# The last twelve attention slots of a linear-attention and cosine-MLP kernel: 64 tokens of two batches instead of 128 tokens of one

## The chip, the core and the metric

The kernel runs on one core of a Trainium2 chip. The time is the device time of one execution in microseconds (us). Three executions of the kernel before took 512.67, 513.03 and 513.1 us, a median of 513.03 us. The engines that matter are TensorE (PE in the profile, its weight loads PEld), VectorE (DVE), ScalarE (ACT), GpSimd (POOL) and SyncE (SP), which issues most DMAs. The two on-chip memories are SBUF and PSUM; PSUM has 8 banks, and matmuls write only there.

## The reference

Four batches of eight heads, 768 tokens, head size 48. A linear attention with a decaying state runs along the tokens, and its output, 3072 tokens by 384 features, goes through an MLP with 2048 inner features and the gate h·cos(h):

```python
for t in range(S):
    kt, vt, rt = (k[:, :, t], v[:, :, t], r[:, :, t])
    cur = np.einsum('bhd,bhe->bhde', u[None] * kt, vt)
    y[:, :, t] = np.einsum('bhd,bhde->bhe', rt, state + cur)
    state = w[None, :, :, None] * state + np.einsum('bhd,bhe->bhde', kt, vt)
...
h = x @ w_in
g = h * np.cos(h)
return (g @ w_out).astype(np.float32)
```

All inputs are float32. The tokens of a batch are chained by the state; the four batches don't depend on each other.

## The kernel before

**Slots.** The 3072 tokens are cut into 24 slots of 128 tokens. Slot `i` holds chunk `i // 4` of batch `i % 4` (`chunk`, L656). Within a slot the recurrence is done with matmuls. Keys and queries are scaled by powers of the decay relative to the middle of the chunk (`decT_k`, `decT_r`), so that the product of a key and a query carries the right power of `w`. For one slot TensorE does:

- `mm_a` (L814, matmul L819): for each of four head pairs `p` and both heads `j` of a pair, scores of 128 keys by 128 queries, with a contraction over 48 numbers. The two heads lie in different halves of the array's rows. VectorE's `mask` (L826) then copies the scores above the diagonal over a diagonal matrix that ScalarE has written (`diagonal`, L809: the bonus `u`).
- `mm_x` (L835, matmul L840): 12 matmuls of the queries with the state, each giving 32 output features, in four column parts of the array.
- `mm_x2` (L844, matmul L853): 16 matmuls of the masked scores with the values, again 32 features each.
- `mm_z` (L871, matmul L875): 8 matmuls of scaled keys and values, which give the slot's addition to the state. VectorE's `state` (L927) adds and scales it; the last chunk of a batch needs none.

All of these are float32 matmuls, and each of them is two MATMUL instructions in the profile. The result is split into a high and a low part (`xh`, `xl`) for the MLP.

**Early and late slots.** Slots 0 to 11 (`i < XS`, `XS = 12`) transpose keys and queries on TensorE (L730). Slots 12 to 23 are "late": they are worked off between matmuls of the MLP. Their keys and queries come through staging buffers `raw` with four DMAs each (`load_s`, L690), are transposed by VectorE in 32x32 blocks (L738) and scaled by GpSimd (L743). Late slots issue `mm_x`, `mm_x2` and `mm_z` as one run on TensorE (`mm_xz`).

**The MLP.** Eight blocks of three slots (384 tokens). A step does one group of 128 inner features of a block: 9 float32r matmuls 128x128 by 384 columns for `h` (`mm_h`, L316), the cosine gate on ScalarE and VectorE, and 9 matmuls of the same size for the output (`mm_o`, L322). There are 128 steps, so 2304 such matmuls. Blocks 0 to 3 go in four rounds over parts of the features, blocks 4 to 7 go through all 16 groups at once. A block's first step needs all three of its slots.

**PSUM.** Banks 0 to 2 hold the outputs of the MLP (`B_ACC`), 3 and 4 the values `h` (`B_H`; in blocks 0 to 3 also bank 5, `B_HX`), 5 to 7 the attention (`B_ATT`). Early slots may use all but bank 2 (`B_EARLY`).

**What sets the order.** Every operation is an `Op` with an engine, a due time, a cost and the buffers it uses. `Plan.order` runs 61 passes of list scheduling with changed due times, replays each order with jittered costs, and keeps the one that ends first. Instructions are then issued in that order: an engine's order is fixed when the program is built. `Tile` is one buffer, `Buf` a use of one, and `_free_at` tells when a buffer is free. Of the operations that can start at the same time, an engine takes the one that is due first; it does not leave itself idle for one that is due earlier but starts later. SP's order holds also for its DMAs: one that waits for a buffer holds up those behind it.

## Time and profile before

| | |
|---|---|
| median of three executions | 513.03 us |
| the profiled execution | 512.26 us |
| its span, first to last instruction | 510.5 us |
| TensorE busy | 501.5 us (98%) |
| VectorE busy | 381.0 us (75%) |
| ScalarE busy | 331.0 us (65%) |
| GpSimd busy | 177.1 us (35%) |
| mean granted TensorE clock | 0.999 |

The busy time of TensorE is the time in which at least one matmul is recorded as running. Matmuls overlap, so their durations add up to more than the span; how long one holds up the next is seen from the starts of neighbouring rows in the timeline. A row of the timeline gives the start, the time from the first start to the last end, the engine, line and operation, and the number of instructions merged into the row. In the notation `48*128 48x128` the first pair is rows by columns of the array that are in use, the second the partitions and columns of the moving operand.

### The profile page before, as it was taken

The page shows a single profiled execution, that of the slowest core. Times are in us where ns is not written, and L with a number is a line of the kernel's source. Part 1 is how long each engine was busy: PE and PEld are TensorE (multiplying, and loading weights), DVE is VectorE, ACT ScalarE, POOL GpSimd, SP SyncE. Part 2 cuts the span into 40 slices and gives each one's busy share as a digit, 9 for nine tenths or more (in the row PEclk, how much of TensorE's full clock was granted, in tenths as well). Part 3 has the DMA queues.
Part 4 walks back from the last instruction along what each step waited for, and adds up shares of the span by engine and source line. Part 5 has one row for each costly group of instructions (what it writes and reads, how often), then busy time and mean ns, then how long its engine had stood idle before and what let it go on. Part 6 is the DMA issues. An engine that isn't in the chain of part 4 may idle for free.

```text
span 510.5 us, 11742 instructions
## 1 busy us (share of the span) xinstructions
PE 501.5 (98%) x4389; PEld 480.0 (94%) x4389; DVE 381.0 (75%) x773; ACT 331.0 (65%) x833; POOL 177.1 (35%) x184
## 2 busy tenths in 40 slices
PE   8999999999999999999999999999999999999995
PEld 5788899999999999999999999999999999999995
DVE  6898999888888875576777777777777767756553
ACT  2989987767667756556657465575665765655453
POOL 6777422445454451242426224224044041300000
PEclk9999999999999999999999999999999999999999
DMA  8999226586666593524676736446455465200001
GB/s 137 179 179 190 79 86 218 152 167 156 157 140 131 127 180 44 76 65 67 160 146 151 159 99 167 111 156 152 105 130 140 142 170 114 89 16 33 1 1 49
DMA packets 114975, 61.56 MB, mean 121 GB/s; under 512 B 78433, under 2 KB 110818, under 8 KB 114914
## 3 DMA queue, kind: packets, MB, share of 16 engines
q1 hardware_dynamic: 109586, 53.50, 42.7%
q0 software_dynamic: 5184, 7.08, 9.9%
q8 instruction: 35, 0.57, 0.5%
q14 instruction: 26, 0.21, 0.2%
q10 hardware_dynamic: 144, 0.20, 0.1%
HBM read 48.96 MB, written 11.80 MB: 119 GB/s over the span
## 4 chain that ended last, share of the span: by engine, by line
PE 94%; DMA 2%; DVE 1%; ACT 1%; issue 1%; POOL 0%; SPq 0%; DVEq 0%; POOLq 0%; ACTq 0%
PE bank L322 41%; PE bank L316 39%; PE bank L819 4%; PE bank L853 4%; PE bank L840 3%; PE bank L875 2%; PE bank L730 1%; DMA v<-in_v_dram 1%; DMA k<-in_k_dram 1%; ACT A L809 1%; PE bank L1094 0%; DVE pq L440 0%; POOL f L765 0%; DVE a L800 0%; DVE rq L447 0%
## 5 line engine op out<-in xcount | busy, mean ns | idle before, releaser
L322 PE MATMUL bank<-w_out_hi,gh 128*128 128x384 f32 x384 | 131.9, 344 | 0.0
L322 PE MATMUL bank<-w_out_hi,gl 128*128 128x384 f32 x384 | 129.8, 338 | 0.0
L316 PE MATMUL bank<-xh,w_in_lo 128*128 128x384 f32 x384 | 129.7, 338 | 0.0
L322 PE MATMUL bank<-w_out_lo,gh 128*128 128x384 f32 x384 | 129.5, 337 | 0.0
L316 PE MATMUL bank<-xh,w_in_hi 128*128 128x384 f32 x384 | 129.1, 336 | 0.0
L316 PE MATMUL bank<-xl,w_in_hi 128*128 128x384 f32 x384 | 128.8, 335 | 0.0
L330 DVE SCALAR_TENSOR_TENSOR f<-bank,qi 128x384 f32<-128x384 f32 (+1 forms) x132 | 71.4, 543 | 47.0 <-ACT qi L327 46.5
L327 ACT ACTIVATE qi<-bank 128x384 int32<-128x384 f32 (+1 forms) x132 | 62.8, 479 | 57.7 <-PE bank L316 57.0
L1033 ACT CAST gh<-f 128x384 fp32r<-128x384 f32 (+1 forms) x132 | 65.7, 500 | 48.9 <-DVE f L1030 46.9
L1030 DVE TENSOR_TENSOR f<-bank,f 128x384 f32<-128x384 f32 (+1 forms) x132 | 71.2, 542 | 32.5 <-ACT f L333 30.3
L1036 DVE TENSOR_TENSOR gl<-f,gh 128x384 fp32r<-128x384 f32 (+1 forms) x132 | 80.7, 613 | 19.6 <-ACT gh L1033 19.1
L333 ACT ACTIVATE f<-f 128x384 f32<-128x384 f32 (+1 forms) x132 | 67.3, 513 | 41.6 <-DVE f L330 40.8
L322 PEld LDWEIGHTS bank<-w_out_hi,gh 128*128 128x128 f32 x384 | 72.0, 188 | 3.0 <-issue 0.8
L316 PEld LDWEIGHTS bank<-xh,w_in_lo 128*128 128x128 f32 x384 | 72.2, 188 | 0.3 <-DVE w_in_lo L631 0.3
L316 PEld LDWEIGHTS bank<-xh,w_in_hi 128*128 128x128 f32 x384 | 72.2, 188 | 0.3 <-issue 0.2
L316 PEld LDWEIGHTS bank<-xl,w_in_hi 128*128 128x128 f32 x384 | 72.1, 188 | 0.0
L322 PEld LDWEIGHTS bank<-w_out_hi,gl 128*128 128x128 f32 x384 | 72.1, 188 | 0.0
L322 PEld LDWEIGHTS bank<-w_out_lo,gh 128*128 128x128 f32 x384 | 72.0, 188 | 0.0
L809 ACT ACTIVATE A<-ident,a 128x128 f32<-128x128 f32 x192 | 59.6, 391 | 4.9 <-DVE a L800 4.8
L743 POOL TENSOR_TENSOR kT<-kT,decT_k 112x512 f32<-112x512 f32 x12 | 15.6, 1301 | 129.3 <-DVE kT L738 74.4
L621 POOL TENSOR_TENSOR f<-f,raw 128x384 int32<-128x384 int32 x32 | 36.7, 1148 | 60.8 <-DVE f L610 31.7
L1078 POOL DMA_DIRECT2D out_dram<-f x36 | 32.7, 1012 | 40.6 <-DVE f L1030 17.2
(88 smaller groups left out, 589.5 us busy)
## 6 DMA issues: line engine op xcount, KB each, us to landing
raw<-in_moe_w_in_dram SPq DMA_DIRECT2D x32, 384.0 KB, 3.2
raw<-in_moe_w_out_dram SPq DMA_DIRECT2D x32, 384.0 KB, 3.2
out_dram<-f POOLq DMA_DIRECT2D x36, 192.0 KB, 4.5
k<-in_k_dram SPq DMA_DIRECT2D x24, 192.0 KB, 4.2
v<-in_v_dram SPq DMA_DIRECT2D x24, 192.0 KB, 5.1
raw<-in_k_dram SPq DMA_DIRECT2D x47, 96.0 KB, 3.1
raw<-in_r_dram SPq DMA_DIRECT2D x47, 96.0 KB, 2.1
out_dram<-f SPq DMA_DIRECT2D x23, 192.0 KB, 1.9
```

The costliest lines, as they stand in the source:

```text
L316: nc.tensor.matmul(ph, a, b_, start=(i == 0), stop=(i == len(mm) - 1))
L322: nc.tensor.matmul(acc, a[:, ts], b_[:, f, :], start=(first and i == 0), stop=(last and i == 2))
L327: nc.scalar.activation(qi, ph, AF.Copy, scale=INV_2PI, bias=0.25)
L330: nc.vector.scalar_tensor_tensor(q, ph, INV_2PI, qi, op0=ALU.mult, op1=ALU.subtract)
L333: nc.scalar.activation(q, q, AF.Sin, scale=TWO_PI, bias=0.5 * math.pi)
L621: lambda: nc.gpsimd.tensor_tensor(ai(), ai(), cn(), op=ALU.add),
L809: nc.scalar.activation(A[j]()[:, p, :], ident, AF.Copy, scale=ab()[:, h : h + 1])
L819: nc.tensor.matmul(cube(Ap[j])[:, p, :], kT()[ps, p, :], rT()[ps, p, :], start=True, stop=True)
L1030: nc.vector.tensor_tensor(g()[:, cs], ph()[:, cs], q()[:, cs], op=ALU.mult)
L1033: nc.scalar.copy(gh()[:, cs], g()[:, cs])
L1036: nc.vector.tensor_tensor(gl()[:, cs], g()[:, cs], f32(gh())[:, cs], op=ALU.subtract)
L1078: nc.gpsimd.dma_start(dst, ob(), accum_op=ALU.add)
```

## The change

The twelve late slots get a function of their own, `late_chunk`. A late slot now holds 64 tokens of two batches, `2m` and `2m + 1`, where `m` alternates between slots: slot 12 is tokens 384 to 447 of batches 0 and 1, slot 13 the same tokens of batches 2 and 3, slot 14 tokens 448 to 511 of batches 0 and 1, and so on. In a half of the partitions (`half[b]`) lie the tokens of one batch. The number of slots, and the 384 columns that each block of the MLP streams, stay as they are.

- The score matmuls of a slot become 16 of 48x64 with 64 moving columns, in four parts of the array (head `j` by batch `b`). The addition to the state becomes 16 matmuls of 64x64, also in four parts. Both are issued as one run, `mm_az`. Ten late slots compute an addition to the state instead of eight.
- The matmuls with the state become 24 of 112x32 with 64 moving columns, those with the values 32 of 64x32 with 64 moving columns, in eight parts of the array; their order is written out in `rounds`. They are one run, `mm_xx`.
- The two PSUM buffers of a slot, `sp` (scores and state) and `xp` (output), are pairs of banks, 5 and 6 or 6 and 7 (`P_ATT`), since the parts in different rows of the array write different banks. The planner learns of buffers made of parts (`Tile.parts`).
- Masks and diagonals are 64 columns wide (`upper2`, `ident2`, made once by GpSimd in `start_late`); the state of two batches is one tensor and is updated in two operations on 384 columns instead of 192.
- Staged loads take eight DMAs instead of four, the other loads two instead of one; the number of bytes is the same.
- The table `dec_k` is made a second time for the 64-token slots (`late_table`: eight matmuls of 128x64 and a copy), after all early slots have used the first. `wr` shares the memory of `dec_k`.
- The early slots keep their code; the last of them scale the state to the middle of a chunk of 64.

```diff
+    CT = C // 2
...
-        bank = [Tile(banks.tile([P, 512], F32, name=f"bank{i}")) for i in range(8)]
+        bank_all = banks.tile([P, 8, 512], F32, name="bank")
+        bank = [Tile(bank_all[:, i]) for i in range(8)]
+        P_ATT = [Tile(bank_all[:, i : i + 2], bank[i : i + 2]) for i in (5, 6)]
...
-        zc = [att.tile([KP, NP, D], F32, name=f"zc{b}") for b in range(B)]
-        R_zt = ring("zt", 2, [KP, NP, 2 * D], F32)
-        wr = att.tile([NP, 2, DP], F32, name="wr")
+        zc = [att.tile([KP, 2, NP, D], F32, name=f"zc{m}") for m in range(NM)]
+        zt = att.tile([KP, 2, NP, 2 * D], F32, name="zt")
+        R_zt = [Tile(zt[:, n]) for n in range(2)]
+        R_zt2 = [Tile(zt, R_zt)]
...
+        wr = dec_k.rearrange("q h d -> q (h d)")[0:NP, 0 : 2 * DP].rearrange("q (j d) -> q j d", j=2)
...
+        def start_late():
+            nc.gpsimd.tensor_tensor(ident2, ident[:, 0:CT], ident[:, CT:C], op=ALU.add)
+            nc.gpsimd.tensor_copy(upper2[0:CT], upper[0:CT, 0:CT])
+            nc.gpsimd.tensor_copy(upper2[CT:P], upper[CT:P, CT:C])
...
+        o_late = op(POOL, 60, 0.6, start_late, [o_pool, o_pool2], port=True)
...
+        def late_table():
+            b_tab2 = Buf(B_ATT)
+
+            def tab_t2():
+                pt = b_tab2().rearrange("q (p t) -> q p t", p=NP)
+                for p in range(NP):
+                    for b in range(2):
+                        nc.tensor.matmul(pt[b * CT : (b + 1) * CT, p, :], decT_k[:, p, mid], ident, start=True, stop=True)
+
+            def tab_copy2():
+                pt = b_tab2().rearrange("q (p j d) -> q (p j) d", p=NP, j=2)
+                nc.scalar.copy(dec_k, pt[:, :, 0:D])
+
+            o_t2 = op(PE, 110, 0.5, tab_t2, [o_tt], [b_tab2], lat=0.3)
+            return op(ACT, 110.5, 0.45, tab_copy2, [o_t2, *early_kd], [b_tab2])
...
+            if i >= XS:
+                return late_chunk(i, due, xbuf)
...
-            def mm_xz():
+            def mm_xx():
                 if c:
                     mm_x()
                 mm_x2()
-                if more:
...
+        def late_chunk(i, due, xbuf):
+            if not o_dk2:
+                o_dk2.append(late_table())
+            m, n_ = (i - XS) % NM, (i - XS) // NM
+            t0 = EC * C + n_ * CT
+            kb, vb, mb, ab, rb = Buf(R_k), Buf(R_v), Buf(R_f), Buf(R_a), Buf(R_f)
+            ks, rs = Buf(R_raw), Buf(R_raw)
+            kT, rT = Buf(R_kT), Buf(R_rT)
+            A = [Buf(R_A) for _ in range(2)]
+            sp, xp, zb = Buf(P_ATT), Buf(P_ATT), Buf(R_zt2)
+            half = [slice(b * CT, (b + 1) * CT) for b in range(2)]
+            more = i < NJ - NM
...
+                def go():
+                    for n in range(4):
+                        for b in range(2):
+                            if i < NJ - 1 or n < 3 or b == 0:
+                                part(n, b, 0, 16, 0, NP, 4 * D)
...
+            ahead = [last_A[0]]
+            l_ks = op(SP, due - 6.2, 3.9, load_s(ks, k), ahead, [ks], lat=3.0, line="late")
+            l_rs = op(SP, due - 6.1, 3.9, load_s(rs, r), ahead, [rs], lat=3.0, line="late")
+            l_k = op(SP, due - 5.2, 1.3, load(kb, k), ahead, [kb], lat=2.6, line="late")
+            l_r = op(SP, due - 5.1, 1.3, load(rn, r), ahead, [rb], lat=2.6, line="late")
+            l_v = op(SP, due - 5.0, 1.3, load(vb, v), ahead, [vb], lat=2.6, line="late")
...
+            def mm_az():
+                for p in range(NP):
+                    for j in range(2):
+                        ps = slice(j * DP, j * DP + D)
+                        for b in range(2):
+                            nc.tensor.matmul(
+                                score(j)[half[b], p, :],
+                                kT()[ps, p, half[b]],
+                                rT()[ps, p, half[b]],
+                                start=True,
+                                stop=True,
+                            )
+                if not more:
+                    return
+                z = z_of()
+                for p in range(NP):
+                    for j in range(2):
+                        for b in range(2):
+                            nc.tensor.matmul(
+                                z[j * DP : j * DP + DP, b, p, :],
+                                kb()[half[b], 2 * p + j, :],
+                                vb()[half[b], 2 * p + j, 0:D],
+                                start=True,
+                                stop=True,
+                            )
+
+            last_A[0] = o_A = op(
+                PE,
+                due - 1.7,
+                1.3 if more else 0.75,
+                mm_az,
+                [e_k, e_r] + ([o_kd, l_v] if more else []),
+                [kT, rT, sp] + ([kb, vb] if more else []),
+                lat=0.3,
+            )
+
...
+                    w_c = pq[0:KP, None, :, 15:16].to_broadcast([KP, 2, NP, D])
+                    nc.vector.tensor_tensor(zc[m], z_of()[0:KP], zc[m], op=ALU.add)
+                    nc.vector.tensor_tensor(zc[m], zc[m], w_c, op=ALU.mult)
+
+                last_z2[m] = op(DVE, due - 1.2, 1.2, state, [o_A, *o_zt, *before, o_pow], [sp])
...
+            def mm_xx():
+                x = xp()[:, :, 0 : NK * CT].rearrange("q b (kk t) -> q b kk t", kk=NK)
+                for kk in range(NK):
+                    for b in range(2):
+                        for g in range(4 * kk, 4 * kk + 4):
+                            p, s = divmod(g, 3)
+                            gs = slice(G * (g % 4), G * (g % 4) + G)
+                            nc.tensor.matmul(
+                                x[gs, b, kk, :],
+                                zb()[:, b, p, G * s : G * s + G],
+                                rT()[0:KP, p, half[b]],
+                                start=(kk == 0),
+                                stop=False,
+                                skip_group_check=True,
+                            )
+
+                rounds = (
+                    ((0, 0), (1, 0), (2, 0), (3, 0)),
+                    ((4, 0), (1, 1), (6, 0), (7, 0)),
+                    ((4, 1), (5, 0), (10, 0), (7, 1)),
+                    ((8, 0), (9, 0), (10, 1), (11, 0)),
                 )
+                for group in rounds:
+                    for b in range(2):
+                        for g, n in group:
+                            p, s = divmod(g, 3)
+                            gs = slice(G * (g % 4), G * (g % 4) + G)
+                            parts = {0: ((0, 0),), 1: ((0, G), (1, D)), 2: ((1, DP + 16),)}[s]
+                            j, at = parts[n]
+                            nc.tensor.matmul(
+                                x[gs, b, g // 4, :],
+                                vb().rearrange("q h d -> q (h d)")[half[b], p * 2 * DP + at : p * 2 * DP + at + G],
+                                A[j]()[half[b], p, 0:CT],
+                                start=False,
+                                stop=(n == len(parts) - 1),
+                                skip_group_check=True,
+                            )
+
+            xo = op(PE, due - 0.7, 1.8, mm_xx, [e_r, l_v, *e_A, *o_zt], [rT, xp, vb, zb, *A], lat=0.3)
...
```

More of the change, by code (lines that the diff above doesn't have):

```diff
@@ L95, in _free_at @@
     def _free_at(tile):
-        if tile.owner is None:
-            return 0.0
-        if any(o.end is None for o in tile.owner.users):
-            return None
-        return max(o.end + o.lat for o in tile.owner.users)
+        t = 0.0
+        for x in tile.parts:
+            if x.owner is None:
+                continue
+            if any(o.end is None for o in x.owner.users):
+                return None
+            t = max(t, max(o.end + o.lat for o in x.owner.users))
+        return t
     def _ready(self, o):
@@ L110, in _ready @@
             for tl in b.tiles:
-                if id(tl) in taken:
+                if any(id(x) in taken for x in tl.parts):
                     continue
@@ L117, in _ready @@
                 return None
-            taken.add(id(best[1]))
+            taken.update(id(x) for x in best[1].parts)
             picks.append((b, best[1]))
@@ L136, in latest @@
             for b in o.bufs:
-                owners = tiles.setdefault(b.tile, [])
-                if not owners or owners[-1][0] is not b:
-                    if all(b is not x for x, _ in owners):
-                        owners.append((b, o))
+                for part in b.tile.parts:
+                    owners = tiles.setdefault(part, [])
+                    if not owners or owners[-1][0] is not b:
+                        if all(b is not x for x, _ in owners):
+                            owners.append((b, o))
         for owners in tiles.values():
@@ L156, in replay @@
             for b in o.bufs:
-                if owner.get(b.tile) is not b:
-                    prev[b] = owner.get(b.tile)
-                    owner[b.tile] = b
-                if prev.get(b) is not None:
-                    t = max(t, max(end[d] + d.lat for d in prev[b].users))
+                if b not in prev:
+                    prev[b] = [owner[x] for x in b.tile.parts if x in owner]
+                    for x in b.tile.parts:
+                        owner[x] = b
+                for a in prev[b]:
+                    t = max(t, max(end[d] + d.lat for d in a.users))
             if o.eng != "PE":
@@ L202, in one_pass @@
                 for tl in b.tiles:
-                    tl.owner = None
+                    for x in tl.parts:
+                        x.owner = None
         nxt, left = {}, {}
@@ L234, in one_pass @@
             for b, tl in picks:
-                b.tile, tl.owner = tl, b
+                b.tile = tl
+                for x in tl.parts:
+                    x.owner = b
             o.gap = t - free[o.eng]
@@ L787, in chunk @@
                 o_kd = op(e2, due - 2.7, c2, decay_k, [o_m, o_dk], [kb], port=True)
-            if not first and not late:
+            early_kd.append(o_kd)
+            if not first:
                 t_k = op(PE, due - 2.5, 0.49, tr(kTp, kb), [o_kd, o_pool], [kb, kTp, kT], lat=0.3)
@@ L935, in chunk @@
-                if not late:
-                    zo = op(PE, due + 1.2, 0.5, mm_z, [o_kd, l_v, o_A], [kb, vb, zp], lat=0.3)
-                last_z[b] = op(
-                    DVE, due + 1.4, 0.3 if c == 0 else 0.65, state, [zo, *o_zt, last_z[b], o_pow], [zp]
-                )
+                    w_c = pq[0:KP, None, :, 15:16].to_broadcast([KP, 2, NP, D])
+                    nc.vector.tensor_tensor(zc[m], z_of()[0:KP], zc[m], op=ALU.add)
+                    nc.vector.tensor_tensor(zc[m], zc[m], w_c, op=ALU.mult)
@@ new lines, in late_chunk, with xv, xo_ @@
+            xo = op(PE, due - 0.7, 1.8, mm_xx, [e_r, l_v, *e_A, *o_zt], [rT, xp, vb, zb, *A], lat=0.3)
+            def xv():
+                return xp()[:, :, 0 : NK * CT].rearrange("q b (kk t) -> q kk b t", kk=NK)
+            def xo_(n):
+                return xbuf()[n].rearrange("q kk (b t) -> q kk b t", b=2)
+            x_h = op(ACT, due - 0.4, 0.47, lambda: nc.scalar.copy(xo_(0), xv()), [xo], [xp, xbuf])
+            x_l = op(
+                DVE,
+                due - 0.2,
+                0.55,
+                lambda: nc.vector.tensor_tensor(xo_(1), xv(), f32(xo_(0)), op=ALU.subtract),
+                [x_h],
+                [xp, xbuf],
+            )
@@ L1057 @@
                     jc = FIRST[n] + t
-                    row = (jc % B) * S + (jc // B) * C
-                    dst = out[row : row + C, :]
+                    if jc < XS:
+                        row = (jc % B) * S + (jc // B) * C
+                        dst = out[row : row + C, :]
+                    else:
+                        m, at = (jc - XS) % NM, EC * C + (jc - XS) // NM * CT
+                        dst = out.rearrange("(b s) d -> b s d", b=B)[2 * m : 2 * m + 2, at : at + CT, :]
                     def cp(acc=acc[t], ob=ob, t=t):
```

226 lines of the change are left out of this document (131 added, 95 removed).

## The prediction

> **What bounds the kernel now.** I read the page first, then busy times by stretch, then the chain of waits, and last the timeline of TensorE around one late slot. From the page:
>
> ```profile
> span 510.5 us, 11742 instructions
> PE 501.5 (98%) x4389; PEld 480.0 (94%) x4389; DVE 381.0 (75%) x773; ACT 331.0 (65%) x833; POOL 177.1 (35%) x184
> ```
>
> The busy time of each engine by stretch (columns: time and count of TensorE, its weight loads, VectorE, ScalarE, GpSimd, then clock, DMA share, GB/s):
>
> ```profile
> 0.00:20.00 20.00, 16.66 (x204) 12.32 (x206) 14.09 (x34) 10.23 (x30) 14.43 (x30) 1.00 0.97 146
> 20.00:60.00 40.00, 39.63 (x765) 34.04 (x763) 36.58 (x70) 37.08 (x110) 28.86 (x28) 1.00 0.87 153
> 60.00:460.00 400.00, 400.00 (x3172) 388.82 (x3171) 304.74 (x611) 260.92 (x642) 133.81 (x127) 1.00 0.54 129
> ```
>
> From 60 to 460 us, where all late slots lie, TensorE is never without a matmul. A busy TensorE needn't be at its peak, so I compare starts. Two rows of the chain of waits that are one step of the MLP apart, and in it nothing else:
>
> ```profile
> 146.18 1.58 PE bank L322 x9
> 149.32 1.58 PE bank L322 x9
> ```
>
> A step is 3.14 us for 18 matmuls, 0.174 us from start to start. Against this the timeline of TensorE around slot 18 (start, time from first start to last end, number of instructions):
>
> ```profile
> 341.71 0.34 PE L322 MATMUL bank<-w_out_lo,gh 128*128 128x384 f32 x1
> 341.98 1.16 PE L819 MATMUL bank<-rT,kT 48*128 48x128 f32 x16
> 343.07 0.44 PE L322 MATMUL bank<-w_out_hi,gh 128*128 128x384 f32 x1
> 343.36 0.34 PE L322 MATMUL bank<-w_out_hi,gl 128*128 128x384 f32 x1
> ...
> 346.15 0.34 PE L322 MATMUL bank<-w_out_lo,gh 128*128 128x384 f32 x1
> 346.42 0.86 PE L840 MATMUL bank<-rT,zt 112*32 112x128 f32 x24
> 347.10 1.08 PE L853 MATMUL bank<-A,v 128*32 128x128 f32 x32
> 348.11 0.56 PE L875 MATMUL bank<-v,k 128*48 128x48 f32 x16
> 348.61 0.45 PE L322 MATMUL bank<-w_out_hi,gh 128*128 128x384 f32 x1
> 348.89 0.34 PE L322 MATMUL bank<-w_out_hi,gl 128*128 128x384 f32 x1
> ```
>
> The reader is to see that the attention sits as two runs between matmuls of the MLP, with no wait in brackets behind any of them. So time that a run no longer takes from TensorE comes off the end, as long as no other engine becomes late. A run's price is the distance between the MLP matmul before it and the second one after it, less two MLP steps of 0.174 (the first matmul after a run is also followed late). The scores cost 343.36 - 341.71 - 0.35 = 1.30 us, the second run with the state's addition 348.89 - 346.15 - 0.35 = 2.39. One of the last four slots, which have no such addition:
>
> ```profile
> 384.92 0.34 PE L322 MATMUL bank<-w_out_lo,gh 128*128 128x384 f32 x1
> 385.19 0.86 PE L840 MATMUL bank<-rT,zt 112*32 112x128 f32 x24
> 385.87 1.08 PE L853 MATMUL bank<-A,v 128*32 128x128 f32 x32
> 386.88 0.45 PE L322 MATMUL bank<-w_out_hi,gh 128*128 128x384 f32 x1
> 387.17 0.33 PE L322 MATMUL bank<-w_out_hi,gl 128*128 128x384 f32 x1
> ```
>
> That is 387.17 - 384.92 - 0.35 = 1.90. All twelve late slots cost 8 x (1.30 + 2.39) + 4 x (1.30 + 1.90) = **42.3 us** of TensorE.
>
> **What a run costs after.** The terms are the time from one round to the next (a round is one instruction on every part of the array) and the fixed time around a run. Mean durations of single instructions, from the groups by line and form:
>
> ```profile
> L819 PE MATMUL bank<-rT,kT 48*128 48x128 f32 x384 | 27.6, 284 | 0.3 <-ACT kT L790 0.2
> L853 PE MATMUL bank<-A,v 128*32 128x128 f32 x768 | 26.8, 275 | 0.9 <-DVE A L826 0.8
> L840 PE MATMUL bank<-rT,zt 112*32 112x128 f32 x480 | 17.2, 277 | 0.0
> L875 PE MATMUL bank<-v,k 128*48 128x48 f32 x320 | 11.1, 212 | 0.2 <-DMA v<-in_v_dram 0.2
> ```
>
> A float32 matmul is two instructions (L819: 24 slots x 8 matmuls, 384 instructions). The run of L840 has 24 instructions on four column parts, 6 rounds: (0.86 - 0.28) / 5 = 0.117 us a round for 128 moving columns. L853 gives (1.08 - 0.275) / 7 = 0.115, the scores, two parts, (1.16 - 0.284) / 7 = 0.125. L875, two parts and 48 moving columns, gives (0.56 - 0.21) / 7 = 0.050. So a round is nearly proportional to the columns. A round with 64 isn't in the trace; it lies between 0.050 and 0.117, and on the line between them at 0.050 + 16/80 x 0.067 = **0.063**, which I take, since 64 is nearest to 48.
>
> Around a run: 0.27 into it (341.98 - 341.71); out of it, from its last instruction's start, 0.15 after L875 (348.61 - 348.46) and 0.20 after L853 (386.88 - 386.68), so 0.16 for 64 columns; 0.29 to the next matmul (343.36 - 343.07); less 0.35: 0.37. Where a run changes the shape of the parts I take 0.16 as for the way out.
>
> - Scores and state in one run, 64x64 parts, four at once: 32 + 32 instructions are 8 rounds at 0.063 and 8 at 0.050, 15 steps: 0.50 + 0.35 + 0.37 = 1.22. Without the state: 7 x 0.063 + 0.37 = 0.81.
> - Output run: 48 instructions of 112x32 on four column parts, 12 rounds, then 64 of 64x32 on eight parts, 8 rounds: 11 x 0.063 + 0.16 + 7 x 0.063 + 0.37 = 1.66. The matmuls with the state gain nothing (12 rounds of 0.063 for 6 of 0.117), since their 112 rows leave no second half; the gain is in the scores and in the values.
>
> Ten slots at 2.88 and two at 2.47 make **33.7 us**, 8.6 less than before.
>
> **What it adds.** The second `dec_k` is 8 matmuls of 128x64, two parts, 8 rounds of 0.117: 0.27 + 0.82 + 0.20 + 0.29 - 0.35 = 1.2 us if it lies in dense work, nothing if the list scheduler puts it where TensorE has nothing else. The latter is likely: it needs only the first table, and the rows just behind that show gaps filled by warm-up matmuls (L1094):
>
> ```profile
> 8.11 0.66 PE L472 MATMUL bank<-ident,decT_k 128*128 128x128 f32 x4 [0.69 <-DVE decT_k L456]
> ...
> 9.30 0.49 PE L1094 MATMUL bank<-warm 128*128 128x256 bf16 x3
> 10.09 0.62 PE L730 MATMUL bank<-ident,r 128*112 128x128 f32 x4 [0.30 <-DMA r<-in_r_dram]
> ```
>
> I take 0.6. But there it would hold one of seven early PSUM banks until its copy, which waits for the last early `decay_k`:
>
> ```profile
> 54.20 1.02 POOL L773 TENSOR_TENSOR k<-k,dec_k 128x384 f32<-128x384 f32 x1
> ```
>
> The early part gets a new order in any case, as the search sees other operations. What it can gain is bounded by TensorE's idle time, 3.3 us in the first 20 and 0.4 in the next 40; I allow 0.5. What it can lose has no row; a loss as large as all of that idle time is 3.7. I take 1.3 of loss, between the ends.
>
> **What lies beside TensorE.** In 60 to 460 us VectorE is busy 76%, ScalarE 65%, GpSimd 33%, and TensorE waits for none of them. The operations that answer to the changed ones, in 230 to 450 us:
>
> ```profile
> L809 ACT ACTIVATE A<-ident,a 128x128 f32<-128x128 f32 x85 | 26.6, 390 | 1.3 <-DVE a L800 1.3
> L826 DVE COPY_PREDICATED A<-upper,bank 128x512 f32<-128x512 int32 x22 | 15.0, 735 | 2.1 <-PE bank L819 2.0
> L919 DVE TENSOR_TENSOR xl<-bank,xh 128x384 fp32r<-128x384 f32 x11 | 6.0, 549 | 1.3 <-ACT xh L914 1.3
> L932 DVE TENSOR_TENSOR zc<-bank,zc 112x192 f32<-112x192 f32 x7 | 2.5, 355 | 3.4 <-PE bank L875 3.4
> ```
>
> Masks of half the width save VectorE some 24 x 0.3 = 7 us, and the wider state (two operations of 0.55 as L919 in ten slots for two of 0.355 in eight) adds 11.0 - 5.7 = 5. Diagonals get shorter, spreads longer, GpSimd does as many operations and 0.6 us once. At no cost, hidden behind TensorE. SP issues more:
>
> ```profile
> 378.58 1.76 SPq L693 DMA_DIRECT2D raw<-in_k_dram  x4
> ...
> 384.74 0.38 SPq L672 DMA_DIRECT2D k<-in_k_dram  x1
> ...
> 402.94 2.44 SPq L693 DMA_DIRECT2D raw<-in_k_dram  x4
> ```
>
> Eight staged DMAs for four are 3.5 us instead of 1.75, twice a slot, and three more loads of some 0.5: 5 us more in the 24 between two slots. Behind them queue the raw weights of the range check, whose result TensorE turns (L555) at 465.63, 45 us before the end:
>
> ```profile
> 465.63 0.27 PE L555 MATMUL bank<-ident,fine 128*1 128x128 f32 x1
> ```
>
> So these 45 us cover it; if they didn't, SP's 12 x 5 us would appear.
>
> **The sum.** The profiled execution took 512.26 us, 0.77 below the median shown. 512.26 - 8.6 + 0.6 + 1.3 = 505.6; on the median's scale **506.3 us**.
>
> **Rivals.**
>
> *The parts don't run at once (slower).* No row has halves of the rows and of the columns in use together. For full overlap speaks that each alone works: the four column parts of L840 take 0.32 us together where one takes 0.277, and the first two instructions of L819, on the two row parts, 0.38 where one after the other would take 0.57:
>
> ```profile
> 346.42 0.32 PE L840 MATMUL bank<-rT,zt 112*32 112x128 f32 x4
> ...
> 341.98 0.38 PE L819 MATMUL bank<-rT,kT 48*128 48x128 f32 x2
> ```
>
> If four 64x64 parts went like two and eight 64x32 like four, scores, state and values would need 8 rounds more each: 8 x (0.063 + 0.050 + 0.063) = 1.41 in ten slots, 1.01 in two, 16.1 us in all: 522.4. It decides once 6.7/16.1 = 42% of that overlap is missing. The Trainium skill (TensorEngine Tiling (Array Packing), Tiling Modes) has tiles load weights and multiply independently in every mode, which is the forecast's side; no row of this trace shows the mixed modes. Chance 5%.
>
> *A larger fixed part in every instruction.* Over a full slot 26 steps are 64-column rounds, 310 over all slots, so each 0.01 us on a round costs 3.1. The scores' round, 0.125, is 0.008 above L840's; if all 64-column rounds have that on top, 0.071, the sum loses 2.5: 508.8. The gain is gone at 0.063 + 6.7/310 = 0.085. Against it stands L875's 0.050, where two parts of 48 columns leave 0.01 beside the moving columns. Chance 8%, at 509. The Trainium skill (TensorEngine Tiling (Array Packing), Instruction Overhead) warns of just this, some 60 cycles per matmul, and advises not to tile a dimension that is already small; at the 2.4 GHz that its page Trainium Kernel Development and Optimization gives (NeuronCore Architecture) that is an estimated 0.025 us, by which 64 columns would take 0.071 and 48 columns 0.060. The trace's 0.050 is below that, and the measurement decides.
>
> *A new wait for PSUM.* Both pairs of banks contain bank 6, so the output run can't start before masks and state update have read the scores' pair. VectorE's part of that is two masks of some 0.4 and two operations of 0.55, 1.9 us, and the MLP takes most of VectorE beside it. Today 3.35 us lie between the two runs (343.07 to 346.42). The planner can place the output run a step later at no cost, since slots are some 20 us apart; only where VectorE is later than planned does TensorE stand. At 0.7 us in ten slots the gain is gone: 513. Chance 7%.
>
> *The early part loses more*, by the held bank or a worse draw of the search: 3.7 us instead of 1.3, 508.7. Chance 12%.
>
> **How the numbers follow.** Forecast 68%, the rivals 5, 8, 7 and 12%. The range: downward, rounds at 0.050 would give 310 x 0.013 = 4.0 more, and the table and the early part 1.9; both ends at once are unlikely, and about half of them gives 503.4. Upward it takes in the fixed part and the early loss together with a little of a wait: 511.0. A difference of 0.2%, 1.0 us, is about what a measurement of this kernel can tell from no change. Slower are the first rival and half of the third with a rest: 9%; within 0.2% the other half: 4%; faster 87%.
>
> **What would show it.** Right: runs of `48*64` with 64 columns beside `64*64`, 1.2 us by the same distance; output runs of `112*32` and `64*32`, 1.66 us; no bracket behind either; TensorE busy throughout from 60 us on; late slots at 34 us in all. Wrong: 16 rounds where I count 8; rounds far from 0.063; a wait for VectorE ahead of the output run; MLP matmuls that stop for the gate; the first step of the MLP's steady part later than before by more than 2 us, which puts it on the early part; the check's matmul near the end.

## The result and the profile after

The changed kernel takes 550.76 us in the median of six executions (548.43 to 551.95), against 513.07 (512.67 to 513.32) for the kernel before: a ratio of 1.0736, 95% interval 1.0719 to 1.0752. The forecast was 506.3 in a range up to 511.0, so it is wrong by its sign. The profiled execution took 550.94 us, its span is 549.2, 38.7 more than the 510.5 before.

**The runs on TensorE came out nearly as forecast.** From the timeline of TensorE after, a run of scores and state, then an output run:

```profile
370.51 0.34 PE L331 MATMUL bank<-xh,w_in_lo 128*128 128x384 f32 x1
370.78 0.69 PE L1040 MATMUL bank<-rT,kT 48*64 48x64 f32 x32
371.30 0.63 PE L1053 MATMUL bank<-v,k 64*64 64x48 f32 x32
371.86 0.44 PE L337 MATMUL bank<-w_out_hi,gh 128*128 128x384 f32 x1
372.14 0.34 PE L337 MATMUL bank<-w_out_hi,gl 128*128 128x384 f32 x1
...
375.98 0.34 PE L337 MATMUL bank<-w_out_lo,gh 128*128 128x384 f32 x1
376.25 0.88 PE L1102 MATMUL bank<-rT,zt 112*32 112x64 f32 x48
377.06 0.86 PE L1124 MATMUL bank<-A,v 64*32 64x64 f32 x64
377.85 0.44 PE L337 MATMUL bank<-w_out_hi,gh 128*128 128x384 f32 x1
378.12 0.34 PE L337 MATMUL bank<-w_out_hi,gl 128*128 128x384 f32 x1
```

By the prediction's distance, 372.14 - 370.51 - 0.35 = 1.28 us (forecast 1.22) and 378.12 - 375.98 - 0.35 = 1.79 (forecast 1.66). Without the state a run costs 0.83 (forecast 0.81). Where no wait stands beside them, twelve slots cost 10 x (1.28 + 1.79) + 2 x (0.83 + 1.79) = 35.9 us: 6.4 less than before, where 8.6 were forecast.

**But TensorE is no longer busy throughout.** The waits of TensorE (engine, buffer and line, what was waited for; us in total, times, longest), after:

```profile
PE bank L331 <- DVE f L1240: 9.3, 6, 5.5
PE bank L1102 <- DVE A L1072: 7.3, 4, 2.5
PE bank L815 <- ACT kT L786: 1.9, 2, 1.2
...
PE bank L1040 <- POOL rT L987: 1.2, 2, 1.0
```

Before, TensorE had no wait after 60 us. Now the MLP waits for the gate's product (L1240) and the output run for the masked scores (L1072). Both are VectorE's, which is busy only 70% of the span. So VectorE was held up itself. To see where, I compare the start of the k-th of the 2304 MLP matmuls in the two traces (after minus before, us):

```
k            145    865   1009   1441   1513   1657   1801   1873   2089   2304   end of span
difference  +2.96  +2.93  +1.71  +1.74  +4.98  +6.71  +8.99  +17.5  +25.9  +27.4       +38.7
```

The early part loses 3.0 us. From the 865th to the 1441st matmul the difference falls only by 1.2. Then there are steps up at 340 to 360, 405 to 430 and 475 to 500 us, which lie just behind the ends of blocks 4, 5 and 6, and 11.3 us come after the last matmul. At those four places the output is stored. DMA traffic from 530 us to the end, after (GB/s in 40 slices, packets, then the queue of ScalarE's one store):

```profile
GB/s 0 0 34 0 0 0 13 13 62 46 29 25 41 51 48 51 48 51 51 48 48 52 45 51 51 51 51 51 51 48 48 51 51 38 13 0 0 0 0 0
DMA packets 394, 0.63 MB, mean 33 GB/s; under 512 B 6, under 2 KB 390, under 8 KB 390
...
q10 hardware_dynamic: 130, 0.20, 2.7%
```

The same view before, from 500 us to the end:

```profile
GB/s 0 0 0 0 0 0 0 0 0 0 0 0 0 0 62 0 0 0 0 0 0 316 392 223 398 345 408 146 18 35 49 12 0 0 0 0 0 0 0 0
DMA packets 436, 0.63 MB, mean 60 GB/s; under 512 B 48, under 2 KB 432, under 8 KB 432
...
q10 hardware_dynamic: 144, 0.20, 5.3%
```

The last three stores, nearly all of the 0.63 MB in both, move at some 50 GB/s instead of up to 400. The queue's packets tell why: 144 are 128 rows and 16 packets of 4 bytes; 130 are 128 rows and 2 such packets. The store is one DMA into `out[2m:2m+2, at:at+64, :]` (L1273), whose outermost dimension is 2, and it runs on **2 DMA engines of 16**: from 536 to 543 us, where only the stores move, the 16 engines are busy 0.13 of the time on average, which is two of them. The Trainium skill states this rule (DMA: Bandwidth & Descriptors, Why a DMA increments its semaphore by 16 and not by 1): the number of engines is the largest up to 16 that divides the slowest dimension of both sides that isn't 1. The trace agrees. Neither this line of the diff nor that rule had a place in the prediction.

What a slow store does in the middle of the kernel is shown by the chain of waits after, around the end of block 6:

```profile
478.50 0.51 SPq L1290
479.01 0.05 issue
479.06 9.97 DMA f<-in_w_dram
489.06 0.36 DVE f L543
...
490.49 0.55 DVE f L1240
491.03 0.04 issue
491.08 3.25 PE bank L331 x9
494.32 2.62 PE bank L337 x9
496.94 1.57 PE bank L331 x9
```

A load of 1.5 KB, the flag of the range check (L539), takes 10 us. It is issued behind three stores, whose packets end at 488.6 us, and lands as they end; in the run below with the stores in two, VectorE doesn't wait for it at all. VectorE's next operation in its order works on that flag (L543), the gate's product stands behind it, and TensorE behind that. Elsewhere VectorE waits for the stores' buffer itself (first two lines; the third is the flag):

```profile
DVE f L578 <- DMA out_dram<-f: 6.2, 3, 3.7
...
DVE f L345 <- DMA out_dram<-f: 5.7, 5, 1.9
DVE f L543 <- DMA f<-in_w_dram: 5.7, 1, 5.7
```

And the longer stalls are paid a second time: after the 5.5 us wait in this chain nine matmuls take 3.25 and 2.62 us instead of 1.57. The granted clock says so (busy times by stretch, clock third from the end):

```profile
405.00:430.00 25.00, 17.36 (x245) 15.59 (x246) 13.57 (x29) 11.80 (x33) 4.23 (x4) 0.90 0.45 121
...
490.00:500.00 10.00, 8.92 (x37) 8.93 (x38) 5.56 (x12) 3.85 (x8) 0.00 (x0) 0.68 0.01 2
```

From 490 to 500 us TensorE has 0.68 of its speed, where from 60 to 215 it had 1.00. Not every stall does this: from 340 to 360 us, where no gap on TensorE was above 1.8 us, the clock stayed at 1.00.

### The profile page after: what moved, and what is told of

Same layout as the page of the kernel before. It is cut to its first block, busy times and chain, and to the rows that moved or that the text cites. A ratio compares the mean times of both kernels' runs of the same rounds, so it can differ in the third digit from the quotient of the medians.

```text
span 549.2 us, 14159 instructions
## 1 busy us (share of the span) xinstructions
PE 507.0 (92%) x5464; PEld 480.3 (87%) x5464; DVE 386.6 (70%) x777; ACT 331.6 (60%) x834; POOL 176.1 (32%) x186
## 5 line engine op out<-in xcount | busy, mean ns | idle before, releaser
L331 PE MATMUL bank<-xh,w_in_hi 128*128 128x384 f32 x384 | 131.3, 342 | 9.3 <-DVE f L1240 9.3
L1246 DVE TENSOR_TENSOR gl<-f,gh 128x384 fp32r<-128x384 f32 (+1 forms) x132 | 83.8, 637 | 23.0 <-ACT gh L1243 22.2
L1240 DVE TENSOR_TENSOR f<-bank,f 128x384 f32<-128x384 f32 (+1 forms) x132 | 70.9, 540 | 33.6 <-ACT f L348 32.1
L667 POOL TENSOR_TENSOR f<-f,raw 128x384 int32<-128x384 int32 x32 | 35.0, 1093 | 61.0 <-DVE f L656 40.2
L567 ACT ACTIVATE f<-raw 128x384 f32<-128x384 f32 x32 | 17.6, 551 | 25.2 <-DMA raw<-in_moe_w_in_dram 6.6
```

The costliest lines, as they stand in the source:

```text
L331: nc.tensor.matmul(ph, a, b_, start=(i == 0), stop=(i == len(mm) - 1))
L567: lambda: nc.scalar.activation(ca(), f32(raw()[:, :, 1]), AF.Abs, accum_out=fine[:, i : i + 1]),
L667: lambda: nc.gpsimd.tensor_tensor(ai(), ai(), cn(), op=ALU.add),
L1240: nc.vector.tensor_tensor(g()[:, cs], ph()[:, cs], q()[:, cs], op=ALU.mult)
L1246: nc.vector.tensor_tensor(gl()[:, cs], g()[:, cs], f32(gh())[:, cs], op=ALU.subtract)
```

## The experiments

### The store

In all diffs `-` is the kernel named, `+` the experiment. **The late stores in two**, one DMA of 64 rows for each batch:

```diff
-                    def st(ob=ob, dst=dst, f0=f0, last=last):
-                        if last:
+                    def st(ob=ob, dst=dst, f0=f0, last=last, jc=jc):
+                        if jc >= XS:
+                            eng = nc.scalar if last else nc.sync
+                            for b in range(2):
+                                eng.dma_start(dst[b], ob()[b * CT : (b + 1) * CT])
+                        elif last:
```

> The changed kernel with one thing undone: each late slot's output store is two DMAs of 64 rows (one per batch) instead of one DMA whose outermost dimension is the 2 batches. Order on every engine as in the changed kernel. Theory A (that store runs on two DMA engines, takes over 10 us instead of 2.5, holds its buffer and everything behind it in those two engines' rings): the waits at the ends of blocks 4, 5 and 6 and the 17 us after the last matmul go, leaving the late runs' measured gain of 42.3 - 35.9 = 6.4 us and the early part's loss of 2.9: a span of 507 us (505.5 to 510), 509 by the clock of the runs. Theory B (SP's 22 DMA issues a slot, 4.2 to 8.3 us for each staged load, make VectorE's transposes and masks late): waits of TensorE for the masks stay, over 530 us.

Measured: 518.48 us (517.89 to 522.23), against 513.7 for the kernel before in the same session; ratio 1.0098, interval 1.0065 to 1.0131. Its store's queue has 160 packets, 128 rows and 2 x 16. So 32.3 of the loss go with the store's shape; but the kernel is still slower than before, and that isn't explained by it.

**The store's shape alone, in the kernel before** (its late rows go out as two interleaved halves, with 2 as the outermost dimension, so that they stand in another order in the output):

```diff
+                    if jc >= XS:
+                        dst = dst.rearrange("(t b) d -> b t d", b=2)
```

> The kernel before, with only the shape of the late slots' stores changed: even rows of a slot as one group and odd rows as a second, outermost dimension 2, same 128 rows and bytes (the output rows of these slots come out in another order than the reference's). Theory A: the store alone costs what the changed kernel lost, three disturbed block ends and a late last store: 530 to 555 us, the last store over 10 us. Theory B: nothing changes, 513 us, within 1.

Measured: 534.43 us (533.2 to 536.69), ratio 1.0382, interval 1.0335 to 1.0429. The shape costs 20.7 us in a kernel in which nothing else is changed. There too TensorE waits for the gate (`PE bank L316 <- DVE f L1030`, 5.2 us in 3 waits), and its last matmul starts 13.5 us late, 4.5 of them in the early part. In the changed kernel the same stores cost half as much again.

**Only the very last store in two**, the one on ScalarE's queue.

> The changed kernel with only the very last store (slot 23) as two DMAs of 64 rows on ScalarE's queue. Theory A: its own 10 us go, but the two SP stores before it (slots 21 and 22), issued 1 us earlier, still run on the same two engines, so the end comes 3 to 11 us earlier, 540 to 548 us, and the block ends stay as they are. Theory B: no change beyond 1 us.

Measured: 547.99 us (546.25 to 549.56), ratio 1.0661, interval 1.0605 to 1.0718. It gains 3 us of the 11 behind the last matmul, since the two stores that SP issues just before are still on two engines. The loss isn't a matter of the tail alone.

### The early part

The first store experiment, with the second table's matmuls held back until all early slots have scaled their keys, so that its PSUM bank isn't held:

```diff
-            o_t2 = op(PE, 110, 0.5, tab_t2, [o_tt], [b_tab2], lat=0.3)
+            o_t2 = op(PE, 110, 0.5, tab_t2, [o_tt, *early_kd], [b_tab2], lat=0.3)
```

> As the run with all late stores in two DMAs, and the matmuls of the second decay table may only start after the last early slot has used the first table, so that they hold no PSUM bank in the early part. If the held bank caused the early loss of 2.9 us, the first dense MLP matmuls come 2 to 3 us earlier and the time is 506 us on the scale of the runs, less 0 to 1.2 for eight matmuls in dense work. If the loss is the new draw of the order search, the early part moves by some other amount, of either sign, up to 3 us.

Measured: 549.38 us (547.93 to 551.29), ratio 1.0671, interval 1.0622 to 1.0721. The 145th MLP matmul is 4.1 us late, not less than the 3.5 with the bank held. But the granted clock from 20 to 30 us was 0.83 here and 1.00 there, so this doesn't settle what the held bank costs. The planner found another order, and that has a fault of its own: SP waits 40.5 us for a `raw` buffer of the range check, the loads of slots 13 to 15 come late behind it, and TensorE waits 13.9 us for `rT`. One added edge cost 31 us here. Two orders of this planner can't be compared as if only the edge differed, and the runs below keep the order where they can.

The early part also varies without any edit. The same kernel before, profiled once more:

> The kernel before unchanged, for a second profile of it. In the first profile the 145th matmul of the MLP starts at 85.8 us; in all kernels since, with the same or another early order, 88.8 to 92.1. If the early part differs between executions, it starts 1 to 5 us later than 85.8 here too; if the orders make the difference, within 0.5 of 85.8.

Measured: 513.13 us, with the 145th matmul 0.63 us later than in the first profile and all others behind it equally late. The kernel with more loads (below), which has the same order, shows 2.8 there, the one with the other store 4.5; orders of the changed kernel show 3.0 to 6.3. The granted clock parts these. From 20 to 30 us it was 0.86 and 0.73 in the two kernels in the old order, and 1.00 in both profiles of the kernel before. The five profiles with the changed kernel's own order (the changed kernel itself, its late stores in two, its last store in two, and below its loads cut to 11 and its rounds swapped) have a clock of 1.00 there and show 3.0 to 4.1; in each of them TensorE waits 1.9 us for `kT` (L786 after), where the kernel before waits 0.2. So most of the 3 us goes with the new order.

### SyncE

With the stores in two, these are the loads of one late slot on SP's queue, and what follows from them on GpSimd and TensorE (start, us, engine, line, operation):

```profile
286.91 4.87 SPq L944 DMA_DIRECT2D raw<-in_k_dram  x8
291.88 4.46 SPq L944 DMA_DIRECT2D raw<-in_r_dram  x8
296.45 1.30 SPq L934 DMA_DIRECT2D k<-in_k_dram  x2
297.85 1.27 SPq L934 DMA_DIRECT2D f<-in_r_dram  x2
...
302.62 1.40 POOL L999 TENSOR_TENSOR f<-f,k 128x384 f32<-128x384 f32 x1 [5.72 <-DMA f<-in_r_dram]
303.98 1.28 POOL L987 TENSOR_TENSOR rT<-rT,decT_r 112x512 f32<-112x512 f32 x1
...
305.31 0.69 PE L1040 MATMUL bank<-rT,kT 48*64 48x64 f32 x32 [0.78 <-POOL rT L987]
```

and in the kernel before, for its slot 20:

```profile
363.41 1.76 SPq L693 DMA_DIRECT2D raw<-in_k_dram  x4
366.39 1.74 SPq L693 DMA_DIRECT2D raw<-in_r_dram  x4
368.23 0.39 SPq L672 DMA_DIRECT2D k<-in_k_dram  x1
369.06 1.27 SPq L688 DMA_DIRECT2D f<-in_r_dram  x1
...
372.88 1.03 POOL L765 TENSOR_TENSOR f<-f,k 128x384 f32<-128x384 f32 x1 [0.64 <-DMA f<-in_r_dram]
373.87 1.30 POOL L743 TENSOR_TENSOR rT<-rT,decT_r 112x512 f32<-112x512 f32 x1
...
380.76 1.16 PE L819 MATMUL bank<-rT,kT 48*128 48x128 f32 x16
```

The loads of a slot are issued only after the score run of the slot before (`ahead`, L717 before, L970 after). So they lie in a loop: scores, SP's issues, landing, transpose, scaling on GpSimd, next scores. Before, the last scaling of a slot ends 12.4 to 14.9 us after the scores of the previous slot, and 4.0 to 9.8 us ahead of its own scores (above: 375.17 against 380.76). With the stores in two it ends 15.0 to 21.2 us after, and twice just 0.05 us ahead of its own scores. SP issues the four loads shown in 12 us, GpSimd waits 5.72 us for the fourth with the scaling of `rT` queued behind, and TensorE waits.

To show that the number of loads does it: **the loads cut to 11 per slot as before**, of 128 tokens of one batch, so that the second half of each late slot holds other data than the reference's:

```diff
-                    for b in range(2):
-                        nc.sync.dma_start(
-                            dst()[half[b], :, 0:D], src[2 * m + b, :, t0 : t0 + CT, :].rearrange("h t d -> t h d")
-                        )
+                    t1 = min(t0, S - C)
+                    nc.sync.dma_start(dst()[:, :, 0:D], src[2 * m, :, t1 : t1 + C, :].rearrange("h t d -> t h d"))
...
-                                part(n, b, 0, 16, 0, NP, 4 * D)
...
+                        part(n, 0, 0, 32, 0, NP, 4 * D)
```

> As the run with all late stores in two DMAs, but each late slot loads with 11 DMAs as the kernel before does (four of 32 partitions per staged tensor, one each for the other three) instead of 22. It reads the same number of bytes, 128 tokens of one batch where 64 of two belong, so the second half of each slot holds other data than the reference's. Order of all other work unchanged. Theory: what that run still loses against the 6.4 us of gain (some 11 us of waits after 250 us in its profile) comes from SP's issue time, back to back from 286 to 350 us; then nearly all of it goes and the time is 507 to 511 us. Rival: the waits come from the shared PSUM bank or from VectorE's longer state update; then the time stays within 3 us of that run's 518.5.

Measured: 510.85 us (510.48 to 512.61), against 513.55; ratio 0.9939, interval 0.9917 to 0.996. With that 7.6 us of the changed kernel are gone, and no wait of TensorE above 0.2 us is left behind the early part. From the 865th to the last MLP matmul it gains 3.66 + 2.23 = 5.9 us against before, close to the 6.4 of the runs. And the reverse, **22 loads per slot in the kernel before**, same order (shown are the staged loads; the other three are cut in halves of 64 partitions):

```diff
-                        part(m, 0, 32, 0, NP, 4 * D)
+                        part(m, 0, 16, 0, NP, 4 * D)
+                        part(m, 16, 16, 0, NP, 4 * D)
```

> The kernel before, with only the late slots' loads cut into 22 DMAs instead of 11 (each staged load in halves of 16 partitions, the other three in halves of 64); same bytes, places and order. If SP's issue time alone costs what it did in the changed kernel (518.5 against 510.9 for 11 loads), the time rises by 3 to 10 us to 517 to 523. Rival (the SP time matters only in the changed kernel's order, where the planner had already counted 3.9 us a staged load): less than 2 us.

Measured: 523.82 us (522.41 to 527.75), against 513.8; ratio 1.021, interval 1.0174 to 1.0246. TensorE gets its waits here too (L322 for ScalarE and VectorE 3.7 us, L316 for the gate 1.3), and the slack ahead of the scores falls to 0.05. So the issue costs about 8 to 10 us, in either kernel.

Two cheaper remedies failed. **The unstaged loads on GpSimd's queue:**

> As the run with all late stores in two DMAs, with the six unstaged loads of a late slot issued by GpSimd instead of SP (planned at 2.2 us a pair). SP theory: SP has 4 us less a slot, its waits shrink, 508 to 514 us. Rival: no change beyond 3 us from 518.5; GpSimd's own descriptor work, some 1 us a DMA, may delay the decays (longer than 518).

Measured: 518.75, 520.54 and 522.99 us, and one execution far off, 971.99, which I leave out and can't explain; ratio 1.0141, interval 1.0079 to 1.0203. In the profiled execution the early part of a new order lost 6.3 us and the late part gained 0.6, where the late part lost 4.6 with the stores in two alone. So the late part did get shorter, but the time as a whole shows no gain, and as this is another order, the gain can't be put down to SP's queue. **The planner told what the loads take** (5.0 instead of 3.9 us for a staged load, 1.2 instead of 0.6 for a store):

> As the run with all late stores in two DMAs; only the planner's costs are changed: 5.0 us instead of 3.9 for a staged load (4.2 to 5.0 measured), 1.2 instead of 0.6 for a late store. If SP's time fits into the schedule and only the plan was wrong, the loads are issued early enough and the time is 508 to 512; if SP has too little time in any order, it stays above 515.

Measured: 530.22 us (530.14 to 531.41), ratio 1.0313, interval 1.0268 to 1.0358. With truer costs the order is worse by 12 us. It is again another order; this says only that truer costs needn't lead the search to a better one.

### The eight parts

The output run was the one that missed its forecast, by 0.13 us. Its 64 instructions on eight parts, by stretch (columns: TensorE, its weight loads, clock; the count is of instructions that ran in the stretch):

```profile
377.05:377.30 0.25, 0.24 (x32) 0.24 (x33) 1.00 0.83 201
377.30:377.55 0.25, 0.25 (x49) 0.25 (x29) 1.00 0.27 65
377.55:377.80 0.25, 0.25 (x31) 0.20 (x24) 1.00 0.62 141
```

The first 32 instructions all start in the first 0.25 us, by their starts in the trace eight each 0.06, as forecast. The other 32 need 0.40 us: after a gap of 0.06 they start 6 and 11, or 16 to 18 ns apart. Whether that hangs on what the second 32 do, or on their place, is told by **the four rounds in the order 3, 4, 1, 2:**

> As the run with all late stores in two DMAs, with the four rounds of the value matmuls in the order 3, 4, 1, 2. In the changed kernel's profile the first 32 of these 64 instructions start 7 ns apart and the last 32 some 17 ns apart. If the instruction stream runs dry (position), the slow half is again the second one, now rounds 1 and 2, and the output run costs 1.79 us as before; if it is the pattern of parts in rounds 3 and 4, the first half is slow. The time is that run's within 2 us in both cases.

Measured: 517.85 us (515.83 to 521.14), ratio 1.0067, interval 1.0042 to 1.0092, the same as before this swap within their spread. The slower half is again the second (0.24 and 0.40 us), and the run costs 1.80 us as before. So it is the place in the run, not the operands: after some 32 instructions on eight parts the next ones start more slowly than the parts could take them. What holds them isn't shown by these traces.

### A version without the two faults

If the 64 tokens of the two batches are interleaved (partition 2t + b), a staged load covers both batches in one DMA with 16 as its outermost dimension, and the store is one DMA with 64 outermost:

```diff
-                        dst = out.rearrange("(b s) d -> b s d", b=B)[2 * m : 2 * m + 2, at : at + CT, :]
+                        dst = out.rearrange("(b s) d -> s b d", b=B)[at : at + CT, 2 * m : 2 * m + 2, :]
...
-                            ap=[[4 * D, n_q], [2 * S * D, n_p], [1, n_d]],
+                            ap=[[4 * D, n_q], [H * S * D, n_b], [2 * S * D, n_p], [1, n_d]],
```

> The changed kernel with the two batches of a late slot interleaved where that needs no second DMA: in the staged tensors the partitions alternate between the batches (source dimensions 16, 2, ...; four DMAs per staged load instead of eight; VectorE's transpose writes the batches apart again), and the columns of x alternate, so that an output store is one DMA with 64 tokens outermost. 14 loads and one store a slot; planned at 2.3 us a staged load. Theory: the stores spread over the DMA engines again, SP keeps up, and the gain of the late runs (6.3 us) is left with the early part's shift of either sign up to 4: 505 to 511 us, under the kernel before. Rival: a store or load of this shape still runs on few engines: over 530 us, or TensorE's waits for the staged loads remain: 515 to 520 us.

Measured: 516.33 us (515.51 to 518.56), against 513.8; ratio 1.0059, interval 1.0038 to 1.008. Up to the 1873rd matmul it makes up 5.2 of the 5.4 us that its early part loses, and then stands for 4 us at 435 to 445. There lie the loads of the last slot, which are nine DMAs each since the last rows of the tensor had been cut off into DMAs of 15 and of 1 row:

```profile
424.89 6.05 SPq L944 DMA_DIRECT2D raw<-in_k_dram  x9
431.05 5.60 SPq L944 DMA_DIRECT2D raw<-in_r_dram  x9
```

**With these as one DMA** that reads 160 instead of 192 elements a row (`-` is the interleaved kernel):

```diff
-                            nc.gpsimd.memset(staged(buf)[96:P, NP - 1, 4 * D - 32 :], 0.0)
-                            for p in range(NP - 1):
-                                part(n, 0, 2, 0, 16, p, 1, 4 * D)
-                            part(n, 0, 2, 0, 15, NP - 1, 1, 4 * D)
-                            part(n, 0, 1, 15, 1, NP - 1, 1, 4 * D)
-                            part(n, 1, 1, 15, 1, NP - 1, 1, 4 * D - 32)
+                            nc.gpsimd.memset(staged(buf)[96:P, :, 4 * D - 32 :], 0.0)
+                            part(n, 0, 2, 0, 16, 0, NP, 4 * D - 32)
```

> The interleaved kernel with the last slot's fourth staged load as one DMA of 16 x 2 x 4 x 160 elements (the columns behind are set to zero by GpSimd), so that no slot has more than 4 DMAs for a staged load; the order of operations is the same. Theory (two defects, the store on two DMA engines and SP's issue time, stand between the forecast and the result): the 4 us stall at 435 to 445 us goes, the last matmul starts within 1 us of that of the kernel before, and the time is 511 to 513.5 us, a ratio of 0.996 to 1.000; the early part keeps its loss of some 5 us, and without it the time would be some 508. Rival (the stall came from the output's or the banks' side and the nine DMAs only stood beside it): it stays, 515 to 517 us.

Measured: **511.15 us** (509.52 to 511.77), against 513.78; ratio 0.9934, interval 0.991 to 0.9957. The page, and the same loads on SP's queue with the scaling and the scores behind them:

```profile
span 510.0 us, 13969 instructions
PE 498.7 (98%) x5464; PEld 476.5 (93%) x5464; DVE 389.2 (76%) x777; ACT 331.4 (65%) x834; POOL 178.3 (35%) x186
```

```profile
423.91 3.86 SPq L944 DMA_DIRECT2D raw<-in_k_dram  x4
427.88 3.52 SPq L944 DMA_DIRECT2D raw<-in_r_dram  x4
...
434.54 1.30 POOL L985 TENSOR_TENSOR rT<-rT,decT_r 112x512 f32<-112x512 f32 x1 [1.97 <-DVE rT L976]
...
440.22 0.69 PE L1038 MATMUL bank<-rT,kT 48*64 48x64 f32 x32
```

The scaling ends 4.4 us ahead of the scores again, and in all slots at least that. The last MLP matmul starts 0.9 us earlier than before, 5.3 us of gain in the late part on an early part that loses 4.4. It is the only kernel here that computes all of the reference and is faster than the one before: by 0.7%, which is little, but its slowest execution is below the fastest of the kernel before (512.99).

## Why the prediction was wrong, step by step

- **The late runs** (8.6 us off the sum): right in kind. Four parts of 64x64 do run at once (scores: 8 rounds in 0.515 us to the first instruction of the state, 0.064 a round, where 0.063 was forecast), and four column parts with 64 columns as well (0.808 for 12 rounds, 0.067). The first rival, parts that don't run at once, is out, and the larger fixed part isn't seen in the 64-column rounds on four parts. Two terms are mis-sized. The larger is "7 x 0.063" for the values on eight parts: the 64 instructions there take 0.79 us with the way out to the MLP, where 7 x 0.063 + 0.15 makes 0.59. The other is the state's "8 at 0.050", taken from two parts: on four parts, by the rows above, (0.63 - 0.22) / 7 makes 0.059 a round of 48 columns, hardly less than with 64, and this is the 0.06 of the scores' run. Together they make 6.4 instead of 8.6.
- **Table and early part** (0.6 and 1.3): together 3.0 measured in the first profile, 3.0 to 4.1 in the five with this order. The table's matmuls run at 9.3 to 10.3 us and cost little beyond their 1.1 us. The size lies within the bounds named, -0.5 to 3.7, near the rival's end; whether a held bank is its cause stays open, since the run that freed it had a lower clock.
- **"What lies beside TensorE. At no cost"**: here the prediction failed, at two steps. First, it went through the loads and the operations of VectorE, ScalarE and GpSimd, but not through the stores. The output of a late slot became a DMA with an outermost dimension of 2, and no term, no bound and no rival stood for it: 32.3 us by the store in two, 11.3 of the profile's 38.7 behind the last matmul and most of the rest in stalls at block ends.
- Second, "5 us more in the 24 between two slots" treated SP's issue as throughput, with the range check's flag, 45 us before the end, as what is late next. What is late next is the slot's own scores. The loads wait for the scores of the slot before, so each us of issue is taken from the 4.0 to 9.8 us that lie between scaling and scores. And a staged load took 4.2 to 5.9 us in most slots, not 3.5. This cost 7.6 us after, 10.0 when put into the kernel before. "If they didn't, SP's 12 x 5 us would appear" was too much in the other direction: TensorE stands only in those slots where the slack is used up.
- **A new wait for PSUM**: no row shows TensorE waiting for the pairs of banks as such. Its wait for masked scores ahead of the output run, 7.3 us, was there, but it went to 1.6 with the stores in two, and no such wait is in the version without the two faults.
- **The stop signs** that the prediction listed did show the failure: MLP matmuls that stop for the gate, a wait for VectorE ahead of the output run, and TensorE not busy from 60 us on. They named effects; none named the output's transfer.

With both faults mended, 511.15 against 513.78 is a gain of 2.6 us where the sum had 6.7. The 4.1 us between them: 2.2 from the late runs and 2.5 from the early part (4.4 lost, 1.9 forecast) make 4.7; the rest is within what two profiles differ by.

## What to carry to other kernels

When a tile comes to hold several batches, write down for each DMA, stores above all, its outermost dimension before and after: a 2 there put the store on 2 of 16 DMA engines here, and cost five times what the change could gain. An issue queue's time is to be compared not with the average spacing of its work but with the slack in the loop in which it lies: find the dependency that lets the next load start, and the time between the last operation made ready and its use. And count what is queued behind a slow transfer: here a 1.5 KB load for a range check took 10 us, and the MLP stood for 5.5 us behind it.

## What the runs showed that I had not expected

- SP's time for a DMA goes with its shape, not only its number. Of the same bytes, four staged loads of 32 x 4 x 192 elements took 1.73 us at the least and mostly 1.75; eight of 16 x 4 x 192 took 3.6 at the least, the same 0.45 for each DMA, but mostly 4.2 to 5.9 in the changed kernel; and four of 16 x 2 x 4 x 192, with as many DMAs as the first, took 2.5 to 3.9. What lengthens the eight isn't shown.
- After TensorE had stood for 5.5 us its granted clock was lower, 0.68 from 490 to 500 us, and nine matmuls took 3.25 us in place of 1.57: such a wait costs more than its length.
- On eight parts of 64x32 the first 32 instructions take 0.24 us, the next 32 take 0.40. The Trainium skill (TensorEngine Tiling (Array Packing), Tiling Modes) has the tiles of a mode work independently; with four parts the runs here agree, with eight only for the first half of a run.
- One edge added to the plan, and two truer costs, moved the time by 31 and 12 us through the order that the search then chose.
